# Decoding eight instead of four first-layer weight tiles ahead into result buffers, in a fused attention and two-layer kernel

## The chip, the cores and the metric

The kernel runs on 1 core of one Trainium2 chip. The metric is the device time of one execution in microseconds: 1045.17 us, the median of 3 runs (1044.94 to 1045.97).

## The reference

Three stages follow one another. The tokens are 4 batches of 448, the model width is 768 (12 heads of 64).

```python
scores = cap * np.tanh(scale * q @ k.T / cap)      # per batch and head
x = softmax(scores) @ v                            # 1792 x 768
h = np.maximum(x @ w_in, 0.0)                      # 768 -> 2048
x = (h * h) @ w_out                                # 2048 -> 768
# then 8 experts; each token goes to one, 224 tokens each, by its sorted gate logits
out[mask] = np.maximum(x[mask] @ w1[e], 0.0) @ w2[e]
```

All arrays are float32. The routing is greedy over all logits in falling order.

## The kernel before, in words

**Tiling.** Attention runs batch by batch, in 6 pairs of heads per batch (`attention`, from L234). Per pair, PE computes scores (L259, L261), ScalarE (ACT) takes tanh and exp (L263, L264), DVE or POOL adds up the sums (z, L271 to L279), PE multiplies by v into a PSUM tile U named aux (L286) and sums z over partitions (L295). Then comes the normalisation: for batches from 1 on ACT copies z (L298), DVE takes a reciprocal (L299) and multiplies U by it (L301). That last product is kept in `self.norms` for batch 0. There are two aux buffers, for U and for the sum of z in turn.

**The dense layer.** It works in split fp32: each operand is a high and a low part, and three products replace one (`hidden`, L434 to L436; `output`, L491 to L493). `hidden` goes over 16 tiles j of w_in, with 18 products for each tile in each of the 4 batches. For batch 0 the weights arrive as 64-bit words holding floats in a wider form. A tile goes through these steps:

1. `decode` (L351): SP's queue loads the words into one of 3 buffers raw (L356), and three DVE instructions (L360, L361, L362) make float32 of them in a buffer wf.
2. `split_weights` (L387): ACT copies the high part to wh (L391), and POOL (for every sixth tile DVE) subtracts for wl (L392). There are 4 buffers each of wh and wl.
3. PE uses wh and wl; SP's queue stores both to DRAM (L410) for the later batches.

`weights(n)` (L395) is called for tile n of the sequence that is just to be used. It has tiles up to n+3 loaded and decoded (for n below 4, FIRST tiles more) and tiles up to n+2 split. Tiles 0 to 15 are w_in's, and the 24 after them w_out's.

**The buffers of decoded tiles.** Tiles 3 to 2 + FIRST go to buffers g of the first layer's results, of which there are 16; all others take 3 buffers wf in turn:

```python
if 3 <= n < 3 + FIRST:
    wf = self.mp.tile([128, 2 * S], F32, name="g", bufs=NF)[:, :DM]
else:
    wf = self.wts.tile([128, DM], F32, name="wf", bufs=3)
with self.after(self.norms, WAIT[0], n):
    self.decode(wf, (self.wi if m == "i" else self.wo)[j], w)
```

**The order of the work.** A scheduler orders each engine's instructions ahead of time, by simulated readiness and, among ready ones, by the order in which the program traces them. `after` (L364) adds an edge: in the issue order of DVE, the decoding instructions of tile n come behind `norms[WAIT[0][n]]`, the last product (L301) of that pair of heads of batch 0. It holds for instructions on DVE alone; the load on SP's queue is not ordered by it. `run` traces attention of batch 0 first, then merges `hidden(0)` and `attention(1)` in small steps by their progress. From batch 2 on PE's order is as written; up to then the scheduler chooses it. Each engine executes its instructions strictly in the order built, SP's queue its transfers too.

Of the kernel before, what the change touches and what calls it, by code (L numbers as in the profile page):

```python
# [23 lines left out]
HP = NH // 2  # L24
KC = 4
KP = S // KC
WAIT = {3: 1, 4: 2, 5: 3, 6: 4, 7: 4, 8: 5, 9: 5, 10: 5}, {0: 8, 1: 12, 2: 16}
KB = S // 128
ND = DM // 128
DA = 4  # L30
# [18 lines left out]
AHEAD = 12  # L49
PLAIN = 4  # L50
EARLY = 6
FIRST = 4
WB = 4
START, MASK, VOTE, REST, GATHER, LIST = (7.7, 8.0), (1.85, 3.4), (1.0, 2.6), (0.86, 2.2), (11.0, 12.4), (6.0, 10.0)

# [35 lines left out]
class Kernel:  # L91
# [276 lines left out]
    def load_weights(self, n):  # L368
# [5 lines left out]
        if b == 0:  # L374
# [6 lines that stand above are left out]
# [14 lines left out]
    def weights(self, n):  # L395
        while self.loaded < min(n + 4 + (FIRST if n < 4 else 0), len(self.seq)):
            self.load_weights(self.loaded)
            self.loaded += 1
        while self.ready < min(n + 3, self.loaded):
            if self.seq[self.ready][0] == 0:  # L400
                with self.after(self.exps, WAIT[1], self.ready):
                    self.wtile[self.ready] = self.split_weights(*self.wtile[self.ready])
            self.ready += 1
        pair = self.wtile.pop(n)
        b, m, j = self.seq[n]
        if b == 0:
            w = DM if m == "i" else FF // OB
            self.cache[m, j] = [self.dram.tile([128, w], F32, name=f"w{m}{h}{j}") for h in "hl"]
            for t, c in zip(pair, self.cache[m, j]):
                self.nc.sync.dma_start(c, t[:, :w].bitcast(F32))  # L410
        return pair
# [622 lines left out]
```

## Time and profile before

| | |
|---|---|
| median of 3 runs | 1045.17 us |
| the profiled execution, its own time | 1046.55 us |
| its span in the profile | 1044.8 us |
| busy PE, DVE, ACT, POOL | 1030.5, 586.7, 468.6, 246.0 us |
| granted TensorE clock | 0.996 of full speed |

Times in the profile count from the span's start. PE is the matrix engine's products, PEld its weight loads, which overlap them; SPq is SP's queue of transfers. A row of the timeline gives start, duration, engine, line, operation, what is written from what, and the count of merged instructions; brackets give the engine's idle time just before and what ended it.

### The profile page before, as it was taken

The page shows a single profiled execution, that of the slowest core. Times are in us where ns is not written, and L with a number is a line of the kernel's source. Part 1 is how long each engine was busy: PE and PEld are TensorE (multiplying, and loading weights), DVE is VectorE, ACT ScalarE, POOL GpSimd, SP SyncE. Part 2 cuts the span into 40 slices and gives each one's busy share as a digit, 9 for nine tenths or more (in the row PEclk, how much of TensorE's full clock was granted, in tenths as well). Part 3 has the DMA queues.
Part 4 walks back from the last instruction along what each step waited for, and adds up shares of the span by engine and source line. Part 5 has one row for each costly group of instructions (what it writes and reads, how often), then busy time and mean ns, then how long its engine had stood idle before and what let it go on. Part 6 is the DMA issues. An engine that isn't in the chain of part 4 may idle for free.

```text
span 1044.8 us, 15693 instructions
## 1 busy us (share of the span) xinstructions
PE 1030.5 (99%) x5718; PEld 818.7 (78%) x5718; DVE 586.7 (56%) x1131; ACT 468.6 (45%) x725; POOL 246.0 (24%) x184
## 2 busy tenths in 40 slices
PE   9999999999999999999999999999999999999997
PEld 2246655777677777777888888888999999989997
DVE  5996899997222155556411225444637448677552
ACT  6868776544564633464544100101313224435542
POOL 0237684764221222222000100001220201021000
PEclk9999999999999999999999999999999999999999
DMA  7656767799655589987786268668567358467530
GB/s 283 221 219 240 254 213 240 238 318 348 222 180 190 161 291 336 388 297 283 260 308 220 89 199 289 196 191 266 184 210 256 107 184 281 166 204 235 181 120 27
DMA packets 102654, 237.59 MB, mean 227 GB/s; under 512 B 11121, under 2 KB 22033, under 8 KB 102577
## 3 DMA queue, kind: packets, MB, share of 16 engines
q1 hardware_dynamic: 87712, 219.65, 61.6%
q0 software_dynamic: 3424, 11.19, 3.6%
q10 hardware_dynamic: 11440, 5.75, 2.0%
q8 instruction: 45, 0.74, 0.3%
q14 instruction: 33, 0.26, 0.1%
HBM read 194.08 MB, written 42.47 MB: 226 GB/s over the span
## 4 chain that ended last, share of the span: by engine, by line
PE 85%; issue 10%; DVE 2%; ACT 1%; DMA 1%; POOL 1%; POOLq 0%; ACTq 0%
PE big L969 8%; PE acc L434 8%; PE acc L491 8%; PE acc L435 7%; PE acc L436 7%; PE acc L492 7%; PE acc L493 7%; PE aux L286 6%; PE acc L901 6%; PE big L259 5%; PE acc L908 2%; PE big L261 2%; PE aux L706 2%; PE aux L295 1%; PE aux L592 1%
## 5 line engine op out<-in xcount | busy, mean ns | idle before, releaser
L491 PE MATMUL acc<-g,wh 128*128 128x448 f32 x384 | 148.9, 388 | 0.0
L434 PE MATMUL acc<-xh,wh 128*128 128x448 f32 x384 | 146.3, 381 | 0.0
L492 PE MATMUL acc<-g,wh 128*128 128x448 f32 x384 | 139.9, 364 | 0.0
L435 PE MATMUL acc<-xl,wh 128*128 128x448 f32 x384 | 139.8, 364 | 0.0
L493 PE MATMUL acc<-g,wl 128*128 128x448 f32 x384 | 139.7, 364 | 0.0
L436 PE MATMUL acc<-xh,wl 128*128 128x448 f32 x384 | 139.2, 363 | 0.0
L969 PE MATMUL big<-wh,g 128*112 128x384 f32 x512 | 118.3, 342 | 0.0
L263 ACT ACTIVATE p<-big,isc 128x896 f32<-128x896 f32 x96 | 85.9, 907 | 40.6 <-PE big L259 40.0
L446 DVE TENSOR_TENSOR g<-r,g 128x448 fp32r<-128x448 f32 x58 | 40.6, 701 | 103.2 <-ACT g L445 102.9
L434 PEld LDWEIGHTS acc<-xh,wh 128*128 128x128 f32 x384 | 72.1, 188 | 30.6 <-issue 16.5
L264 ACT ACTIVATE p<-p,capt 128x896 f32<-128x896 f32 x96 | 89.2, 948 | 1.8
L813 POOL DMA_INDIRECT xg<-x,idx x32 | 32.0, 1000 | 245.6 <-DMA wh<-woh 128.3
L969 PEld LDWEIGHTS big<-wh,g 128*112 128x112 f32 x512 | 86.6, 175 | 0.4
L299 DVE RECIPROCAL z<-z 128x448 f32<-128x448 f32 x18 | 53.1, 2949 | 60.1 <-ACT z L298 60.1
L286 PE MATMUL aux<-p,v 128*64 128x448 f32 x384 | 84.8, 552 | 0.1
L491 PEld LDWEIGHTS acc<-g,wh 128*128 128x128 f32 x384 | 73.3, 191 | 11.3 <-issue 5.6
L435 PEld LDWEIGHTS acc<-xl,wh 128*128 128x128 f32 x384 | 72.2, 188 | 7.9 <-issue 3.5
L492 PEld LDWEIGHTS acc<-g,wh 128*128 128x128 f32 x384 | 72.4, 189 | 6.3 <-issue 2.2
L493 PEld LDWEIGHTS acc<-g,wl 128*128 128x128 f32 x384 | 72.0, 188 | 6.0 <-issue 0.7
L436 PEld LDWEIGHTS acc<-xh,wl 128*128 128x128 f32 x384 | 72.0, 188 | 5.8 <-issue 0.7
L441 ACT ACTIVATE r<-acc 128x448 f32<-128x448 f32 x64 | 34.8, 544 | 86.4 <-PE acc L436 86.4
L259 PE MATMUL big<-qk 64*128 64x448 f32 x288 | 71.4, 578 | 1.0 <-ACT p L263 1.0
(191 smaller groups left out, 1820.1 us busy)
## 6 DMA issues: line engine op xcount, KB each, us to landing
g<-w SPq DMA_DIRECT2D x62, 384.0 KB
wh<-wih SPq DMA_DIRECT2D x48, 384.0 KB
wl<-wil SPq DMA_DIRECT2D x48, 384.0 KB
wh<-woh SPq DMA_DIRECT2D x72, 256.0 KB
wl<-wol SPq DMA_DIRECT2D x72, 256.0 KB
wf<-w SPq DMA_DIRECT2D x33, 384.0 KB
raw<-w SPq DMA_DIRECT2D x33, 384.0 KB
raw<-w_in SPq DMA_DIRECT2D x16, 768.0 KB
```

The costliest lines, as they stand in the source:

```text
L259: nc.tensor.matmul(ps[:, s, :S], k[rows], q[rows], start=True, stop=True)
L263: nc.scalar.activation(p, ps[:, :n, :S], AF.Tanh, scale=self.isc)
L264: e = nc.scalar.activation(p, p, AF.Exp, scale=self.capt)
L286: nc.tensor.matmul(U[hp][s * 64:s * 64 + 64], vt[hp][:, c, s * 64:s * 64 + 64], P[hp, c][:, s if c < KB else 0], start=(c == 0), stop=(c = ...
L434: nc.tensor.matmul(ps, wh[:, d], xh, start=(d == 0), stop=False)
L435: nc.tensor.matmul(ps, wh[:, d], xl, start=False, stop=False)
L436: nc.tensor.matmul(ps, wl[:, d], xh, start=False, stop=(d == ND - 1))
L491: nc.tensor.matmul(ps, a, gh, start=(f == 0), stop=False)
L492: nc.tensor.matmul(ps, a, gl, start=False, stop=False)
L493: nc.tensor.matmul(ps, z, gh, start=False, stop=(f == NF - 1))
L901: nc.tensor.matmul(H[j], W[j][0][:, d], xs[:, d, 0].bitcast(F32), start=(d == 0), stop=(d == ND - 1))
L969: nc.tensor.matmul(acc[h][:, s, :DM // 2], l, r[:, s * (DM // 2):(s + 1) * (DM // 2)], start=(j == 0 and first), stop=(j == NF2 - 1 and last))
```

## The change

FIRST rises from 4 to 8. So tiles 3 to 10, not 3 to 6, are decoded into g buffers, and while the first four tiles are in use up to 11 tiles ahead, not 7, are loaded. The three wf buffers are then taken by tiles 0 to 2 and from 11 on (before: from 7 on). WAIT gets entries for tiles 11, 12 and 13: their decoding instructions too are issued behind `norms[5]`, the last L301 of batch 0, as those of tiles 8 to 10 are already.

```diff
-WAIT = {3: 1, 4: 2, 5: 3, 6: 4, 7: 4, 8: 5, 9: 5, 10: 5}, {0: 8, 1: 12, 2: 16}
+WAIT = {3: 1, 4: 2, 5: 3, 6: 4, 7: 4, 8: 5, 9: 5, 10: 5, 11: 5, 12: 5, 13: 5}, {0: 8, 1: 12, 2: 16}
...
-FIRST = 4
+FIRST = 8
```

## Rows read from the trace of the kernel before

**Rows 1.** The page, busy time of each engine over the span.

```profile
PE 1030.5 (99%) x5718; PEld 818.7 (78%) x5718; DVE 586.7 (56%) x1131; ACT 468.6 (45%) x725; POOL 246.0 (24%) x184
```

**Rows 2.** Busy time by stretch; then PE's weight loads of L434, 62 to 172 us.

```profile
core 0: us, PE busy (x) PEld busy (x) DVE busy (x) ACT busy (x) POOL busy (x), PEclk, DMA share, GB/s
62.00:172.00 110.00, 110.00 (x485) 66.85 (x484) 96.21 (x73) 80.97 (x120) 76.54 (x41) 1.00 0.66 226
80.00:100.00 20.00, 20.00 (x91) 13.82 (x89) 12.86 (x8) 18.02 (x29) 18.80 (x11) 1.00 0.65 242
100.00:120.00 20.00, 20.00 (x92) 11.79 (x89) 17.07 (x13) 14.63 (x22) 13.36 (x8) 1.00 0.78 274
...
L434 PEld LDWEIGHTS acc<-xh,wh 128*128 128x128 f32 x96 | 18.0, 188 | 15.6 <-issue 9.5 <-ACT wh L391 2.8 <-ACT p L263 0.7
```

**Rows 3.** Timeline of PE, 62 to 172 us: start, duration, engine, line.

```profile
62.13 0.47 PE L434 MATMUL acc<-xh,wh 128*128 128x448 f32 x1
62.44 0.36 PE L435 MATMUL acc<-xl,wh 128*128 128x448 f32 x1
...
63.44 0.36 PE L434 MATMUL acc<-xh,wh 128*128 128x448 f32 x1
63.73 0.97 PE L286 MATMUL aux<-p,v 128*64 128x448 f32 x4
...
91.44 1.72 PE L286 MATMUL aux<-p,v 128*64 128x448 f32 x6
...
119.02 0.47 PE L434 MATMUL acc<-xh,wh 128*128 128x448 f32 x1
...
171.06 0.47 PE L434 MATMUL acc<-xh,wh 128*128 128x448 f32 x1
```

**Rows 4.** Timeline of DVE, 75 to 125 us.

```profile
75.09 3.72 DVE L362 SCALAR_TENSOR_TENSOR wf<-raw,wf 128x768 int32<-128x768 int32 x2
83.40 2.95 DVE L299 RECIPROCAL z<-z 128x448 f32<-128x448 f32 x1 [4.60 <-ACT z L298]
...
87.18 0.61 DVE L301 TENSOR_TENSOR x<-aux,z 128x448 f32<-128x448 f32 x1
...
94.62 1.50 DVE L360 TENSOR_SCALAR wf<-raw 128x768 int32<-128x768 int32 x1 [2.95 <-POOL wl L392]
...
97.15 2.77 DVE L362 SCALAR_TENSOR_TENSOR wf<-raw,wf 128x768 int32<-128x768 int32 x1
...
101.99 0.55 DVE L360 TENSOR_SCALAR wf<-raw 128x768 int32<-128x768 int32 x1
...
103.57 0.97 DVE L362 SCALAR_TENSOR_TENSOR wf<-raw,wf 128x768 int32<-128x768 int32 x1
...
108.06 0.50 DVE L360 TENSOR_SCALAR wf<-raw 128x768 int32<-128x768 int32 x1
...
109.53 0.95 DVE L361 SCALAR_TENSOR_TENSOR wf<-raw,wf 128x768 int32<-128x768 int32 x1
110.51 2.75 DVE L362 SCALAR_TENSOR_TENSOR wf<-raw,wf 128x768 int32<-128x768 int32 x1
114.97 1.50 DVE L360 TENSOR_SCALAR wf<-raw 128x768 int32<-128x768 int32 x1 [1.70 <-POOL wl L392]
...
118.34 1.78 DVE L362 SCALAR_TENSOR_TENSOR wf<-raw,wf 128x768 int32<-128x768 int32 x1
...
124.30 0.56 DVE L360 TENSOR_SCALAR wf<-raw 128x768 int32<-128x768 int32 x1 [1.74 <-POOL wl L392]
```

**Rows 5.** Timeline of POOL, 96 to 102 us.

```profile
96.18 2.92 POOL L273 TENSOR_TENSOR z<-p,p 128x896 f32<-128x896 f32 x1 [0.48 <-ACT p L264]
99.05 2.54 POOL L392 TENSOR_TENSOR wl<-wf,wh 128x768 fp32r<-128x768 f32 x1
```

**Rows 6.** Timeline of SP's queue, the loads of raw for w_in, 76 to 101 us.

```profile
77.00 2.16 SPq L356 DMA_DIRECT2D raw<-w_in  x2
...
99.94 0.33 SPq L356 DMA_DIRECT2D raw<-w_in  x1
```

## The prediction

> **What bounds the kernel now.** I read the busy table first: the matrix engine (PE) is busy for 1030.5 of 1044.8 us [rows 1]. The change touches only the input weights of the first dense layer, so the stretch that matters runs from the first product with w_in, at 62.13 us, to the last ones at about 172 us [rows 3]. The table by stretch shows PE busy for 110.00 of these 110 us, and for the whole of each 20 us slice in it; the vector engine (DVE) has 12.86 of 20 and 17.07 of 20, and POOL 18.80 of 20 in the slice from 80 us on [rows 2]. The list of waits, cut to this stretch and to PE, is empty. So in this stretch PE waits for nobody, and what DVE does there is hidden unless it comes too late.
>
> A busy share can flatter PE, so I checked the timeline of single products. Between L435 at 62.44 and L434 at 63.44 lie five starts, one every 0.20 us, and each holds a weight load of 0.188 us [rows 2, 3]: within a run of such products PE is full. By the Trainium skill, Perfetto Trace Analysis, Identifying the Most-Contended Engine, matmul busy time is no measure of the distance to the roofline, and the busy share of weight loads is. By that rule the 66.85 of 110.00 us of weight loads [rows 2] would leave 43 us open. The rows speak against using it here: the 0.188 of 0.20 us is full by the rule's own measure, and the share falls because attention's fp32 products hold PE longer for each load. The only irregularity that I find between starts is at the changes from one kind of product to the other; that is the faster rival below.
>
> **What the limit on decoding is now.** A w_in tile is decoded by three DVE instructions. Tiles 0 to 2 and from 7 on use three buffers named wf, so tile n from 10 on waits until tile n-3 has been split. The timeline of DVE shows it: tile 10 begins at 94.62 after 2.95 us of idling for POOL's wl, tile 13 at 114.97 and tile 14 at 124.30 likewise, and tile 11 at 101.99 directly behind the split of tile 8, which ends at 99.05 + 2.54 = 101.59 [rows 4, 5].
>
> **The change, part by part.**
> 1. Tiles 7 to 10 go to g buffers, tiles 11 to 13 to the three wf buffers, free since tiles 0 to 2 were split. So tiles 10, 11, 12 and 13 lose the wait for a split. Tile 14 reuses tile 11's buffer, as it does now, and still waits for the same split, after which it begins at 124.30 [rows 4]. From tile 14 on, the ring of buffers is the old one, and nothing later is decoded earlier. Four decodes move. Tile 7 was in no wait; it only changes its address.
> 2. Work on DVE: none is added. The four moved decodes took 97.15 + 2.77 - 94.62 = 5.30 (tile 10), 103.57 + 0.97 - 101.99 = 2.55 (tile 11), 0.50 + 0.95 + 2.75 = 4.20 (tile 12, with other work between its three instructions) and 118.34 + 1.78 - 114.97 = 5.15 us (tile 13), 17.2 us together [rows 4]. Tile 11's 2.55 us is the price without company; the others ran beside POOL. Bounds for the four: 4 x 2.55 = 10.2 and 4 x 5.30 = 21.2 us. I take 17.2, for POOL is as busy where they go [rows 2].
> 3. What the earlier decode brings PE: nothing. Tile 8 was split at 101.59, and its first product came at 119.02 [rows 3, 5]: 17 us of slack, and the split, not the decode, is what the next tile waits for; it is paced by the products that free wh and wl.
> 4. DMAs: the raw loads of tiles 13 to 16 each follow the decode three before them, so SP issues them earlier (tile 13 now at 99.94) [rows 6]. The order on issue binds DVE instructions only, not the loads. Behind an early raw load on SP stand the stores of split weights, and v and qk loads. The stores free wh and wl, where the 17 us of slack is the cover; the next heads' loads are a whole head ahead. I cost this at nothing; should one of them wait as long as the first pair of raw loads took to issue, 2.16 us [rows 6], the slack covers it.
> 5. The hidden results shift by four g buffers. A result of tile j from 8 on now takes a buffer that held tile 3 to 10, all of them split before tile 11 is; its first use, tile 8's result, comes after 119.02 [rows 3], when tile 3 is long split. I cost it at nothing.
> 6. The order on DVE: tiles 8 to 13 are held behind the last product with a reciprocal of the first attention, so attention of batch 0 is unharmed. They are not held behind anything of batch 1. Loads 8 to 11 are traced before all of batch 1, and 12 and 13 before its first normalisation, so the scheduler prefers them. This is the only place where I see a loss.
>
> The sum: 0 on the path. Against the profiled execution's own 1046.55 us (span 1044.8 [rows 1]) that gives 1046.55; it lies 1.38 us above the median of the runs, so I forecast the median, 1045.2 us. A measurement of this kernel tells some 0.2%, 2.1 us, from no change.
>
> **Rivals.**
> *Slower: the first normalisation of batch 1 waits behind decodes.* Its reciprocal starts at 83.40 and the product L301 ends at 87.18 + 0.61 = 87.79; that frees a PSUM buffer, and the next head's product with v starts on PE at 91.44 [rows 3, 4]. The slack is 3.65 us. DVE is free from 75.09 + 3.72 = 78.81, where tile 9 ends [rows 4]. If tiles 10, 11 and 12 stand ahead of the reciprocal, it starts at 78.81 + 5.30 + 2.55 + 4.20 = 90.86, 7.46 us late: PE, whose order is fixed when the program is built, stands for 7.46 - 3.65 = 3.8 us, and gets none of it back. With two decodes ahead (86.7, 3.3 us late) nothing shows; with four it is 9.0 us; at the price without company three hide (86.5) and four cost 2.0 us. It decides when the third decode is ahead. For it: the trace order; POOL's 18.80 of 20 us. Against: raw tile 12 cannot be fetched before tile 9 is decoded, so it lands after the reciprocal is ready; and the scheduler places PE's products by its own DVE times, so it can put more hidden products in front. I take three: 1045.2 + 3.8 = 1049.0 us. Chance 0.20.
> The row that carries the long prices is tile 10's third instruction, 2.77 us from 97.15, where tile 11's took 0.97; POOL ran z from 96.18 to 99.10 and wl from 99.05 [rows 4, 5]. By the Trainium skill, SBUF — State Buffer, Who interferes with whom, a DVE instruction with two SBUF inputs contends with a POOL instruction that reads SBUF, and the second to start is blocked for the whole of the other. The trace agrees; it is a rule against this change.
>
> *Faster: PE changes kind less often.* Between 62.13 and 171.06 PE starts 29 runs of split-weight products between fp32 ones [rows 3]. Entering one costs 62.44 - 62.13 - 0.20 = 0.11 us, leaving one 63.73 - 63.44 - 0.20 = 0.09, together 0.20. With more tiles ready the scheduler could place runs of a whole tile (18 products): 288 products in 16 runs, 13 fewer, 2.6 us, 1042.6 us. Against: the tiles are ready 17 us ahead already, and the interleaving follows the written merge of the two streams. Chance 0.13.
>
> *The decodes don't move:* the program holds them back elsewhere (raw ring, order). Then the time is 1045.2 as well; it is inside the forecast.
>
> **How the numbers follow.** No change 0.66, faster 0.13, slower 0.21 (the slower rival with 0.01 for a mishap elsewhere). Likeliest time 1045.2. Own range of that case: plus or minus 1.2 us, from six entries more or fewer. The range given reaches to both rivals' prices: 1042.6 to 1049.2; outside it lies the four-decode case, 1045.2 + 9.0 = 1054.2.
>
> **What would show it.** Right: tiles 10 to 13 decoded by about 100 us instead of 120; DVE idles for POOL's wl at tile 14 alone; tile 14 still near 124; PE full from 62 to 172; about 29 runs. Wrong on the slow side: PE idle before L286 near 91 us, released by DVE L301, and the reciprocal of batch 1's first head starting after 90. Wrong on the fast side: clearly fewer runs, or the work of this stretch ending before 170.

## The result and the profile after

The changed kernel takes 1051.86 us (median of 6 runs, 1051.37 to 1053.70), the kernel before beside it 1045.06 us (6 runs, 1044.55 to 1045.97). The ratio is 1.0069, with a 95% interval of 1.0058 to 1.0080: 6.8 us slower, above the forecast and above the upper end of the range. The profiled execution took 1052.11 us with a span of 1050.3 us, 5.5 us longer than that of before.

The page, busy time of each engine, and from its part 5 the group of the first product of a triple, with its idle time behind the second bar:

```profile
PE 1030.3 (98%) x5718; PEld 818.1 (78%) x5718; DVE 587.9 (56%) x1131; ACT 468.8 (45%) x725; POOL 245.7 (23%) x184
...
L434 PE MATMUL acc<-xh,wh 128*128 128x448 f32 x384 | 147.1, 383 | 4.8 <-ACT r L441 4.8
```

No engine has more instructions than before, and none has over 1.2 us more busy time [rows 1]. PE has the same 1030 us to do and stands still in between: 4.8 us before L434, put down to ACT's L441. Busy time by stretch shows where:

```profile
62.00:172.00 110.00, 104.51 (x451) 63.21 (x450) 88.93 (x67) 74.87 (x109) 70.54 (x38) 0.98 0.64 216
80.00:100.00 20.00, 19.08 (x86) 12.36 (x82) 19.86 (x11) 10.99 (x18) 17.40 (x8) 1.00 0.83 270
100.00:120.00 20.00, 16.07 (x67) 10.83 (x67) 11.96 (x11) 15.31 (x24) 9.54 (x6) 0.91 0.78 269
```

PE, busy for all of these stretches before [rows 2], is idle for 5.5 of the 110 us. DVE has gone from 12.86 to 19.86 of 20 us in the slice from 80 on: it is full there, and it has been given work of later tiles. The granted clock, 1.00 before, is 0.91 in the slice from 100 on.

The list of waits says what ended the idle time. PE, 62 to 180 us, in total, times, longest; then ACT, 80 to 106 us:

```profile
PE acc L434 <- ACT r L441: 4.8, 1, 4.8
PE acc L435 <- DVE xl L348: 0.6, 1, 0.6
...
ACT r L441 <- DVE g L446: 11.6, 1, 11.6
```

So there are two steps back from PE: PE waited for ACT, and ACT had itself waited 11.6 us for one DVE instruction, L446. The timeline of DVE shows what stood ahead of it:

```profile
79.86 5.97 DVE L362 SCALAR_TENSOR_TENSOR g<-raw,g 128x768 int32<-128x768 int32 x3
85.75 2.48 DVE L360 TENSOR_SCALAR wf<-raw 128x768 int32<-128x768 int32 x1
88.27 1.79 DVE L361 SCALAR_TENSOR_TENSOR wf<-raw,wf 128x768 int32<-128x768 int32 x1
90.10 2.75 DVE L362 SCALAR_TENSOR_TENSOR wf<-raw,wf 128x768 int32<-128x768 int32 x1
92.77 1.49 DVE L360 TENSOR_SCALAR wf<-raw 128x768 int32<-128x768 int32 x1
94.29 1.78 DVE L361 SCALAR_TENSOR_TENSOR wf<-raw,wf 128x768 int32<-128x768 int32 x1
96.11 2.46 DVE L362 SCALAR_TENSOR_TENSOR wf<-raw,wf 128x768 int32<-128x768 int32 x1
98.49 0.55 DVE L360 TENSOR_SCALAR wf<-raw 128x768 int32<-128x768 int32 x1
98.96 2.94 DVE L299 RECIPROCAL z<-z 128x448 f32<-128x448 f32 x1
101.82 0.89 DVE L361 SCALAR_TENSOR_TENSOR wf<-raw,wf 128x768 int32<-128x768 int32 x1
102.63 0.61 DVE L446 TENSOR_TENSOR g<-r,g 128x448 fp32r<-128x448 f32 x1
103.16 0.61 DVE L301 TENSOR_TENSOR x<-aux,z 128x448 f32<-128x448 f32 x1
```

Tiles 8 to 10 are decoded interleaved and end with the first row, at 85.83. Tile 11 takes the next three rows, tile 12 the three after them, and tile 13's first two instructions surround the first reciprocal of batch 1. Only then comes L446 of tile 1, the low part of the second hidden result (tiles count from 0). In the kernel before, the same L446 stood between the reciprocal and L301:

```profile
86.27 0.99 DVE L446 TENSOR_TENSOR g<-r,g 128x448 fp32r<-128x448 f32 x1
```

ACT had finished its operand at 86.18 there and at 86.33 here, so DVE is 16.4 us late with it.

ACT runs nothing between these two rows of its timeline; the second waits for that L446:

```profile
90.94 0.83 ACT L391 CAST wh<-g 128x768 fp32r<-128x768 f32 x1
103.33 0.55 ACT L441 ACTIVATE r<-acc 128x448 f32<-128x448 f32 x1 [11.56 <-DVE g L446]
```

PE's timeline around the stop; the row at 107.01 is the last of the nine products that follow it:

```profile
98.72 0.36 PE L436 MATMUL acc<-xh,wl 128*128 128x448 f32 x1
103.93 0.74 PE L434 MATMUL acc<-xh,wh 128*128 128x448 f32 x1 [4.85 <-ACT r L441]
104.47 0.57 PE L435 MATMUL acc<-xl,wh 128*128 128x448 f32 x1
104.84 0.57 PE L436 MATMUL acc<-xh,wl 128*128 128x448 f32 x1
...
107.01 0.37 PE L436 MATMUL acc<-xh,wl 128*128 128x448 f32 x1
```

The first and the last of the same nine products in the kernel before, tile 5's first being the row at 97.89:

```profile
97.89 0.36 PE L434 MATMUL acc<-xh,wh 128*128 128x448 f32 x1
...
99.49 0.36 PE L436 MATMUL acc<-xh,wl 128*128 128x448 f32 x1
```

**The chain.** r has two buffers (the code: `name="r", bufs=2`). Tile 3's r needs the buffer that tile 1's L446 still has to read, so ACT's L441 of tile 3 waits 11.56 us. L441 is what empties tile 3's PSUM accumulator, and there are two of those, so the first product of tile 5 can't start. It starts 5.21 us after the product before it, where 0.20 us is the spacing.

**The bill**, each product of after against the same one of before. At 98.72 PE is 1.03 us late (its product stands at 97.69 in before). At 103.93 it is 6.04 late (97.89): the stop cost 5.01. From there to 107.01 eight steps take 3.08 us, 1.60 in before: 1.48 us more, because products now start 0.37 us apart, not 0.20. At 107.01 it is 7.52 late (99.49), and at the last w_in product of batch 0 7.69 (179.86 against 172.17). Of the 1.03 us, 0.15 stand there already at the product at 74.84 (74.69 in before); the rest stems from a second late DVE product, xl (L348, waited for 0.64 us at 77.6), and what is reordered beside it. In a second profile of this kernel, below, that wait is absent and the stop is 5.25 us. Of the 7.69 us, 5.5 are left at the end of the span; where the other 2.2 go is not the same in the two profiles, and stays unexplained.

The order of PE's instructions is the same as before, but for two neighbouring products near 77 us that stand two places earlier. That is the point on which everything below turns.

### The profile page after: what moved, and what is told of

Read it like the earlier page. It is cut to its first block, busy times and chain, and to the rows that moved or that the text cites. A ratio compares the mean times of both kernels' runs of the same rounds, so it can differ in the third digit from the quotient of the medians.

```text
span 1050.3 us, 15688 instructions
## 1 busy us (share of the span) xinstructions
PE 1030.3 (98%) x5718; PEld 818.1 (78%) x5718; DVE 587.9 (56%) x1131; ACT 468.8 (45%) x725; POOL 245.7 (23%) x184
## 4 chain that ended last, share of the span: by engine, by line
PE 81%; issue 8%; DVE 5%; ACT 2%; DMA 2%; POOL 1%; another core or an unknown queue 0%; POOLq 0%; SPq 0%; ACTq 0%
PE big L969 9%; PE acc L491 8%; PE acc L434 7%; PE acc L492 7%; PE acc L493 7%; PE acc L435 7%; PE acc L436 7%; PE acc L901 6%; PE aux L286 5%; PE big L259 4%; PE acc L908 3%; PE aux L706 2%; PE aux L295 1%; PE big L261 1%; DMA raw<-w_in 1%
## 5 line engine op out<-in xcount | busy, mean ns | idle before, releaser
L434 PE MATMUL acc<-xh,wh 128*128 128x448 f32 x384 | 147.1, 383 | 4.8 <-ACT r L441 4.8
L446 DVE TENSOR_TENSOR g<-r,g 128x448 fp32r<-128x448 f32 x58 | 40.7, 702 | 118.5 <-ACT g L445 118.2
L434 PEld LDWEIGHTS acc<-xh,wh 128*128 128x128 f32 x384 | 72.4, 189 | 35.9 <-issue 17.0
L299 DVE RECIPROCAL z<-z 128x448 f32<-128x448 f32 x18 | 53.1, 2949 | 57.5 <-ACT z L298 57.5
L286 PE MATMUL aux<-p,v 128*64 128x448 f32 x384 | 84.8, 552 | 0.1
L441 ACT ACTIVATE r<-acc 128x448 f32<-128x448 f32 x64 | 34.8, 544 | 98.7 <-PE acc L436 86.4
L259 PE MATMUL big<-qk 64*128 64x448 f32 x288 | 71.2, 576 | 1.7 <-ACT p L263 1.7
```

Of the source, the lines that this page charges most:

```text
L259: nc.tensor.matmul(ps[:, s, :S], k[rows], q[rows], start=True, stop=True)
L286: nc.tensor.matmul(U[hp][s * 64:s * 64 + 64], vt[hp][:, c, s * 64:s * 64 + 64], P[hp, c][:, s if c < KB else 0], start=(c == 0), stop=(c = ...
L434: nc.tensor.matmul(ps, wh[:, d], xh, start=(d == 0), stop=False)
```

## Experiments

The theory at the start, A: decodes ahead of L446 of tile 1 on DVE, lengthened by POOL, hold r, hence acc, hence PE. Rivals: the late normalisation (L299, L301) holds PE, as the prediction's slower rival said; the new buffers or the bigger lead in loads cost time by themselves. Each ratio is against the kernel before on the same chip, whose median was 1041.7 to 1044.4 us there. All edits are on the changed kernel unless said otherwise.

**The buffers without the early decoding.** Tiles 3 to 10 go to g buffers, but the lead stays that of before.

```diff
-        while self.loaded < min(n + 4 + (FIRST if n < 4 else 0), len(self.seq)):
+        while self.loaded < min(n + 4 + (4 if n < 4 else 0), len(self.seq)):
```

> Edit: FIRST = 8 for the buffers, but only four tiles more are loaded ahead, as in the kernel before; so tiles 7 to 10 use g buffers and tiles 11 to 13 find wf free, and yet decodes 10 and later are traced behind the hidden results of the tiles before them. Theory A: DVE's order has L446 of the second tile right behind decode 8, ACT and PE never wait: same as the kernel before within 1 us. If the freed buffers themselves (the earlier loads, the places in g) cost something, 2 us or more slower.

1042.97 us, ratio 1.0007 (0.9998 to 1.0017). L446 of tile 1 is at 89.42, and PE waits for nothing between 62 and 180 us. The addresses are harmless; it is the tracing of decodes 8 to 11 ahead of all of batch 1 that moves them to the front of DVE's queue. The three new entries of WAIT do nothing: built without them, the changed program is the same.

**How many tiles ahead.** FIRST is 6, then 7; and the changed kernel again, for its profile on another chip.

```diff
-FIRST = 8
+FIRST = 6
```

> Edit: FIRST = 6 in place of 8, so two tiles fewer are decoded ahead; DVE's order then has decodes 8 to 11 ahead of L446 of the second hidden tile, no longer tile 12 and the start of 13. Theory A: L446 comes some 6 us earlier, which is more than PE's wait of 4.8 us, so no wait for acc remains; the smaller loss of 0.9 us before 80 us (xl L348 behind decodes) stays: 1045 to 1046.5. Rival B: L301 comes 6 us earlier too, near 97, still 9 us later than in the kernel before, so part of the loss stays: 1047 to 1050. Rival C: fewer loads early, 1047 to 1050.

> Edit: FIRST = 7. DVE's order has decodes 8 to 12 ahead of L446 of the second hidden tile, but not the start of 13. Theory A (the results of the second and third tile wait on DVE behind decodes, their two buffers r hold up ACT and that PE): L446 comes 1 to 3 us earlier than in the changed kernel, so PE's wait shrinks from 4.8 to between 2 and 4 us and brings the lower clock again; 3 to 6 us slower than before. With FIRST = 6 nothing was lost: the loss sets in with the decode of tile 12. Rival C (SP's queue): about 3.5 us per step, so also 3.5 us.

> The changed kernel itself, beside the kernel before on the same chip, as the measure for the other runs of this chip. All theories: some 7 us slower than the kernel before, PE's wait of 4.8 us for L441 and the stretch at the lower clock as in its first profile.

FIRST 6: 1041.80 us, 0.9997 (0.9987 to 1.0006). FIRST 7: 1048.41 us, 1.0060 (1.0044 to 1.0077). FIRST 8: 1050.26 us, 1.0074 (1.0057 to 1.0091). L446 and L441 in the timelines, then PE at tile 5's first product, with the stop where there is one; first FIRST 6:

```profile
95.48 1.81 DVE L446 TENSOR_TENSOR g<-r,g 128x448 fp32r<-128x448 f32 x1
97.21 0.61 DVE L301 TENSOR_TENSOR x<-aux,z 128x448 f32<-128x448 f32 x1
97.38 0.55 ACT L441 ACTIVATE r<-acc 128x448 f32<-128x448 f32 x1 [5.76 <-DVE g L446]
98.35 0.36 PE L434 MATMUL acc<-xh,wh 128*128 128x448 f32 x1
```

FIRST 7:

```profile
100.81 0.56 DVE L446 TENSOR_TENSOR g<-r,g 128x448 fp32r<-128x448 f32 x1
102.06 0.74 PE L434 MATMUL acc<-xh,wh 128*128 128x448 f32 x1 [3.94 <-ACT r L441]
```

FIRST 8 a second time:

```profile
103.53 0.74 PE L434 MATMUL acc<-xh,wh 128*128 128x448 f32 x1 [5.25 <-ACT r L441]
```

A step, not a slope. From L446's end to tile 5's first product there are 0.69 us in the changed kernel (103.24 to 103.93), and in before that product starts at 97.89; so L446 may end as late as 97.20. It ended at 87.26: about 10 us of slack. With FIRST 6 it ends at 97.29. Tile 5 begins at 98.35 in that profile, so L446 is 0.37 us inside what is allowed there, and nothing shows. With FIRST 7 it ends at 101.37 and PE stops for 3.94 us. The same run speaks against the late normalisation: with FIRST 6, L301 ends at 97.82, 10 us later than in before (87.79 by [rows 4]), and PE waits for nothing.

**Without POOL's company.** For the first two pairs of heads of batch 1 the sums z are left out: a fill with 1.0 in place of L273, and no L275 and L279.

```diff
-                    nc.gpsimd.tensor_add(z, P[hp, 0], p)
-            elif c == 2:
+                    nc.gpsimd.memset(z, 1.0) if b == 1 and hp < 2 else nc.gpsimd.tensor_add(z, P[hp, 0], p)
+            elif c == 2 and (b != 1 or hp > 1):
...
-            elif c == KB and b:
+            elif c == KB and b and (b != 1 or hp > 1):
```

> Edit: the changed kernel without the adding up of the softmax sums on POOL for the first two pairs of heads of batch 1 (a constant is written instead; this part of the computation is left out). The order on DVE stays. Theory A with POOL as the cause of the long decodes: decodes 8 to 12, which took 26 us beside POOL where 2.5 us each would be 13, get some 5 us shorter, L446 of the second tile comes near 97 us instead of 102.6, and PE's wait of 4.8 us shrinks to 0 to 1: 1045 to 1047.5 us. Rival D (the decodes are long for another reason, such as waiting for raw loads): they keep their lengths, 1051 to 1053.

1041.73 us, 1.0002 (0.9993 to 1.0012): the whole loss is gone. The order on DVE and on PE is that of the changed kernel; only durations differ. First, busy time by stretch in the changed kernel (columns as above), then the same stretch here and DVE's rows of tile 12:

```profile
79.00:99.00 20.00, 20.00 (x90) 12.70 (x88) 19.86 (x13) 11.99 (x20) 17.40 (x8) 1.00 0.78 250
```

```profile
79.00:99.00 20.00, 20.00 (x92) 13.77 (x89) 15.47 (x14) 16.48 (x26) 8.39 (x5) 1.00 1.01 360
...
85.28 1.51 DVE L360 TENSOR_SCALAR wf<-raw 128x768 int32<-128x768 int32 x1
86.83 0.96 DVE L361 SCALAR_TENSOR_TENSOR wf<-raw,wf 128x768 int32<-128x768 int32 x1
87.82 0.96 DVE L362 SCALAR_TENSOR_TENSOR wf<-raw,wf 128x768 int32<-128x768 int32 x1
...
93.14 0.61 DVE L446 TENSOR_TENSOR g<-r,g 128x448 fp32r<-128x448 f32 x1
93.84 0.55 ACT L441 ACTIVATE r<-acc 128x448 f32<-128x448 f32 x1 [3.39 <-DVE g L446]
```

With POOL at 8.39 of 20 us instead of 17.40, tile 11's decode takes 0.89 + 2.49 + 0.96 = 4.34 us and tile 12's 3.43, where they took 7.02 and 5.73. Tiles 8 to 10 end earlier too, at 78.57 instead of 85.83. L446 ends at 93.75, 9.5 us earlier and inside the slack. So the decodes in front of L446 alone are not enough; their lengthening beside POOL is a necessary part. SP's queue has the order of the changed kernel here, so the earlier loads don't cost the 7 us by themselves either. By the Trainium skill, SBUF — State Buffer, Who interferes with whom, a DVE instruction with two SBUF inputs shares a port with a GpSimd instruction that reads SBUF, a tensor_scalar can come to hold that port too, and one with a single input outside those modes does not contend. The traces agree: in the changed kernel L360, L361 and L362 take 0.55, 0.89 and 0.94 us with POOL idle (98.49, 101.82 and 103.70) and up to 2.48, 1.79 and 2.75 beside it, while the reciprocal takes 2.94 us with POOL idle (98.96) and 2.95 beside POOL's sums (83.40 in before) [rows 4].

**More room for r.** In batch 0 r takes the unused buffers of another tile, seven instead of two.

```diff
-            r = mp.tile([128, S], F32, name="r", bufs=2)
+            r = self.tp.tile([128, S], F32, name="xt") if b == 0 else mp.tile([128, S], F32, name="r", bufs=2)
```

> Edit: the changed kernel, with the hidden result r of batch 0 in 7 buffers instead of 2; the order of the instructions on each engine stays that of the changed kernel. Theory A (two buffers r: DVE's subtraction L446 of the second hidden tile stands behind five decodes, so ACT's L441 of the fourth tile waits 11.6 us, so PE waits 4.8 us for a PSUM buffer acc, and then runs some 1.5 us at the lower clock): both go, 1045 to 1046.5 us, although L446 comes as late as before, near 102 us. Rival B (the late normalisation, L299 and L301 of batch 1's first heads, is what costs): they stay late, 1051 to 1053. Rival C (loads issued earlier on SP's queue delay stores and the loads of q, k and v): SP's order stays, 1051 to 1053.

1046.68 us, 1.0049 (1.0032 to 1.0066). L446 is as late as before, at 103.02, but ACT's wait for it and PE's for L441 are gone. In their place PE waits for the next things in DVE's queue:

```profile
107.85 0.47 PE L436 MATMUL acc<-xh,wl 128*128 128x448 f32 x1 [1.96 <-DVE wl L392]
...
104.30 0.97 PE L295 MATMUL aux<-z,ones 128*64 128x448 f32 x4 [0.32 <-DVE x L301]
```

So the chain through r is real, but cutting it gives back only a third of the loss: the expectation was too good. (The profiled execution is the fastest of the four, 1044.57 us. PE's waits between 62 and 180 us, 2.9 us in all, are those of this execution; for the other three, at 1046.57 to 1047.33, there is no trace.) DVE is late as a whole, and wl of tile 6, which is DVE's by the rule of every sixth tile, is the next victim.

**The same, and wl of tile 6 on POOL.**

```diff
-            self.wtile[n] = (wf, w, nc.gpsimd if n % 6 else nc.vector, self.wts, WB)
+            self.wtile[n] = (wf, w, nc.gpsimd if n % 6 or n == 6 else nc.vector, self.wts, WB)
...
-            r = mp.tile([128, S], F32, name="r", bufs=2)
+            r = self.tp.tile([128, S], F32, name="xt") if b == 0 else mp.tile([128, S], F32, name="r", bufs=2)
```

> Edit: the changed kernel with 7 buffers r for batch 0 (as in the first run of this study) and the split of tile 6 on POOL instead of DVE, so that two of the three things that PE was seen to wait for in DVE's queue are taken out of it; DVE's decodes stay, PE's order stays. Theory A2: with r alone 4.7 us were left, of which the profile showed 2.0 us of waiting for wl of tile 6, 0.3 for L301 and 0.9 before 80 us; now 0.5 to 2.5 us slower than before. If the queue of DVE as a whole is not the cause: still 4 to 5 us slower.

1045.96 us, 1.0017 (1.0007 to 1.0027). One wait of PE is left between 62 and 180 us, 0.66 us for xl. With L446 still at 103.01, the loss is down from 0.74% to 0.17%, on another chip: r's buffers and that wl account for most of it.

**L446 of tile 1 on POOL.** If only this instruction is the matter, POOL can do it.

```diff
-            (nc.gpsimd if b == 0 and j % 3 == 0 else nc.vector).tensor_sub(gl, r, gh.bitcast(F32))
+            (nc.gpsimd if b == 0 and (j % 3 == 0 or j == 1) else nc.vector).tensor_sub(gl, r, gh.bitcast(F32))
```

> Edit: the changed kernel, with L446 of the second hidden tile alone on POOL instead of DVE; every other instruction stays where it is. Theory A: POOL takes it at about 89 us, L441 of the fourth tile follows at once, PE's wait of 4.8 us and the low clock go: 1045 to 1047.5 us (the third tile's L446, still on DVE behind the decodes, may hold the fifth tile a little). Rival B: L301 stays near 103 us, 1051 to 1053. Rival C: 1051 to 1053.

1049.60 us, 1.0077 (1.0060 to 1.0093): no gain, and the expectation missed. ACT, then PE:

```profile
107.63 0.54 ACT L441 ACTIVATE r<-acc 128x448 f32<-128x448 f32 x1 [8.94 <-DVE g L446]
108.23 0.74 PE L434 MATMUL acc<-xh,wh 128*128 128x448 f32 x1 [3.85 <-ACT r L441]
```

The wait only moves one tile on: now it is tile 4's L441 that waits, for tile 2's L446, which DVE runs at 105.32.

**Only a late L446.** The kernel before, with a pad of five DVE instructions after which L446 of tiles 1 and 2 is ordered. Nothing is decoded earlier.

```diff
-            (nc.gpsimd if b == 0 and j % 3 == 0 else nc.vector).tensor_sub(gl, r, gh.bitcast(F32))
+            if b == 0 and j == 1:
+                pad = self.tp.tile([128, S], F32, name="xt")
+                nc.vector.tensor_scalar(pad, r, 1.0, None, op0=OP.add)
+                for i in range(4):
+                    last = nc.vector.reciprocal(pad, pad)
+            with self.tc.issue_after(last.ins) if b == 0 and 0 < j < 3 else nullcontext():
+                (nc.gpsimd if b == 0 and j % 3 == 0 else nc.vector).tensor_sub(gl, r, gh.bitcast(F32))
```

> Edit: the kernel before, with an addition and four reciprocals on a spare tile on DVE (some 12.5 us), and L446 of the second and third hidden tile ordered behind the last of them; the normalisation of the first pair of heads, the split of tile 6 and all loads keep their places, and no decode is moved. Theory A: L446 of the second tile comes near 103 us, L441 of the fourth tile waits for it, PE waits 4 to 6 us for acc and then runs at the lower clock: 5 to 8 us slower than the kernel before. Rival B (late normalisation) and rival C (SP's queue): no loss, within 1 us of the kernel before.

1040.96 us, 0.9988 (0.9978 to 0.9997). L446 of both tiles runs at 101.73, nearly as late as in the changed kernel, and PE loses nothing; the expected loss was wrong, and A as it stood with it. PE's timeline shows why:

```profile
98.33 1.72 PE L286 MATMUL aux<-p,v 128*64 128x448 f32 x8
99.89 0.92 PE L295 MATMUL aux<-z,ones 128*64 128x448 f32 x4
100.74 1.02 PE L259 MATMUL big<-qk 64*128 64x448 f32 x4
101.69 1.02 PE L261 MATMUL big<-qk 128*128 128x448 f32 x2
102.64 1.72 PE L286 MATMUL aux<-p,v 128*64 128x448 f32 x8
104.29 0.47 PE L434 MATMUL acc<-xh,wh 128*128 128x448 f32 x1
```

The order built has 6 us of attention here, and tile 5 starts behind it, at 104.29. In the changed kernel tile 5 is next. So the theory had to be revised, to A2: a late L446 costs time only where PE's order was built for an early one. The likely reason, not shown: the pad's reciprocals keep their length beside POOL (2.93 to 2.95 us), so that a scheduler could foresee them, while the decodes of 7.02 and 5.73 us came out longer than it reckoned.

**Attention first.** If A2 holds, an order that puts attention ahead of tile 5 by hand should remove the wait for L441, and show what else DVE holds.

```diff
+            if b == 0 and j == 5:
+                yield 8.0
```

> Edit: the changed kernel, with the merge made to hand out attention's next products ahead of the sixth hidden tile; on PE four products with v, two sums of z and three scores (some 4 us) now stand before that tile's first product, DVE's order up to the second and third tile's L446 stays. Theory A (a late L446 costs by itself): the hidden results come as late as in the changed kernel, so 6 to 8 us slower than before. Theory A2 (it costs because PE's fixed order has the product that needs the buffer next, as the order was built for shorter decodes): the wait for L441 shrinks to about 1 us, but the sums of z need the aux buffer that L301 frees, which ends near 103.7 in the changed kernel: PE waits there for some 3 us instead, and 4 to 6 us slower than before.

1052.76 us, 1.0084 (1.0066 to 1.0102): 8.3 us slower, above the 4 to 6 that A2 gave and the 6 to 8 that A gave, so the time does not decide between them. The waits do: as A2 had it, the wait for L441 is gone from PE, though ACT still waits 11.56 us, and PE waits for L301 instead. PE's timeline:

```profile
103.31 1.32 PE L295 MATMUL aux<-z,ones 128*64 128x448 f32 x4 [3.63 <-DVE x L301]
104.83 1.86 PE L259 MATMUL big<-qk 64*128 64x448 f32 x4 [0.20 <-ACT p L263]
107.11 1.86 PE L261 MATMUL big<-qk 128*128 128x448 f32 x2 [0.43 <-ACT p L263]
```

The attention that now comes first needs L301, which is late as well: the PSUM buffer that it frees is wanted by the next pair's sum of z (L295). Hidden layer and attention are both held up by DVE's queue, so this order is no way out.

**The pad, with PE's order pinned.** The run with the pad alone shows no price for a late L446, since the order moved. Here the kernel with the pad also has the second half of the products with v of the second pair ordered behind tile 5's seventh product.

```diff
-                nc.tensor.matmul(ps, wh[:, d], xh, start=(d == 0), stop=False)
+                mm = nc.tensor.matmul(ps, wh[:, d], xh, start=(d == 0), stop=False)
+                if b == 0 and j == 5 and d == 2:
+                    self.fifth = mm
...
-                pv(hp - 1, 2, 4)
+                with self.tc.issue_after(self.fifth.ins) if b == 1 and hp == 2 else nullcontext():
+                    pv(hp - 1, 2, 4)
```

> Edit: the padded kernel of the run before (the kernel before, with 12.5 us of extra work on DVE ahead of L446 of the second and third hidden tile), and in addition the products with v of the second pair of heads are held on PE behind the sixth tile's seventh product, so that PE's order around the late result is again that of the kernel before. Theory A2: L446 comes near 102, as in the padded kernel, and now PE waits for L441 from 98.5 on, 4 to 5 us, and then runs at the lower clock: 5 to 8 us slower than before, where the padded kernel lost nothing. If neither L446 nor the order is the cause: same as the padded kernel, within 1 us of before.

1045.79 us, 1.0023 (1.0010 to 1.0035): 1.4 us slower, where 5 to 8 were expected. The scheduler put other fp32 products, L295, L259, L261 and the third pair's first L286, in front from 97.95 us on; tile 5 began at 104.11 and PE waited for nothing. The order of before was not obtained, so this tells nothing on A2.

**The faster rival.** The kernel before, with the first batch's hidden layer merged by whole tiles instead of half tiles: 19 runs of split-weight products instead of 28 between 62 and 173 us.

```diff
-                if d == 2:
+                if d == 2 and b:
...
-            yield 1.7
+            yield 1.7 if b else 3.4
```

> Edit: the kernel before, with the merge of the first hidden layer's batch 0 handing out a whole tile (18 products) at a time instead of half a tile; PE then changes 16 times fewer between split-weight and fp32 products, eight entries and eight exits. The faster rival of the prediction prices an entry and an exit at 0.20 us together: 8 x 0.20 = 1.6 us faster than before (0.15 per cent), if nothing else comes late. Against it: if the price of a change is only a shift within the pipeline, no difference; if whole tiles make attention's products late for ACT, up to 1 us slower.

1042.50 us, 1.0005 (0.9996 to 1.0014), where 1.6 us less was expected: fewer changes of kind bring nothing that can be measured in the total. In this one profile the stretch ended earlier (last w_in product at 170.32 us, 172.17 in before on another chip), but at 199.74 PE stands still for 0.94 us, waiting for ACT's L298, which it does not in before. So the price of 0.20 us for a run is neither shown nor excluded; the time that it would give back did not reach the end.

## Why the prediction was wrong

**What held.** The matrix engine was full, and DVE's work was hidden *unless it comes too late*, as the first paragraph said. Step 1 held: from tile 14 on the ring is the old one, and tile 14 was decoded at 129.96, though with L446 ahead of it, not a wait for POOL's wl. Step 3 held: earlier decodes brought PE nothing (FIRST 6, ratio 0.9997). Step 5 held: the shifted buffers are harmless (ratio 1.0007). Step 4 held in the main, but not to nothing: in the changed kernel DVE stood 1.79 us for a raw load at 72.90, ahead of the xl (L348, 76.64 against 71.75 in before) for which PE waited 0.64 us. In the second profile DVE stood 0.89 us for that load, and PE did not wait for xl.

**The step that failed** is step 6, which saw DVE's new order and put it at nothing ("0 on the path", where 6.8 us were measured), and the price of the rival built on it. Step 6 named the right place, batch 1's work on DVE behind decodes of batch 0, and the rival the right sign, the lock between DVE and POOL, and that a threshold decides (FIRST 6 costs nothing, FIRST 7 costs 0.60%). But the forecast stood on the other side, with a chance of 0.20 for the rival, for four reasons:

1. *The wrong victim.* The rival let L301 hold the next product with v, at 91.44 [rows 3], with 3.65 us of slack. In the changed kernel that product ran at 92.47, while L301 came at 103.16: it doesn't need L301's buffer. Products with v and sums of z don't simply take the two aux buffers in turn: a pair's products with v take the buffer of the sum before them, which ACT's L298 frees, and its sum of z (L295) takes the one that L301 frees, as the row with attention first shows. In before that L295 ran at 103.44, 15.65 us after L301's end, so the 7.46 us of the rival would have cost nothing by this path; that its sign came true was luck, as far as this path goes. So of the two signs that the prediction named for the slow side, the late reciprocal appeared and the idling before L286 didn't. The victim was L446, whose 10 us were the smaller slack; the prediction never listed it, though it stood in DVE's timeline between the reciprocal and L301. A list of all that DVE does between 80 and 105 us, each with its reader and the number of its buffers, would have led from L446 to two r buffers, two accumulators and PE.
2. *The price of a decode.* Step 2 took 2.55 to 5.30 us for a tile, and the rival 12.05 us for tiles 10 to 12. Tiles 11 and 12 alone took 12.75 us. In before, tiles stand between other work; put back to back under POOL's 17.4 of 20 us, almost each of their instructions meets a POOL instruction.
3. *The start.* The rival had DVE free from 78.81. There tile 10 was interleaved with 8 and 9, and they ended at 85.83. With the prices this made the reciprocal 15.56 us late (98.96 against 83.40 in [rows 4]) where 7.46 were supposed; 6.0 of the 8.1 us between them are tiles 11 and 12 (12.75 where 2.55 + 4.20 were supposed). L446's end was 15.98 us late (103.24 against 87.26); 9.94 of them were slack, and the other 6.04 are PE's delay at 103.93.
4. *The counterweights.* That raw tile 12 "lands after the reciprocal is ready" doesn't help, since DVE's order is fixed and what is behind a decode waits, ready or not. That the scheduler "can put more hidden products in front" did not happen: it moved PE's order for the pad, but here PE's order stayed the same.

The size of the rival, 3.8 us, was too small beside the 6.8 measured for one more reason: it charged a stop for its length alone. The 5.01 us cost another 1.48 in slower products right behind them. The upper end of the range stood on the rival's price, and so lay too low.

**The faster rival** did not come about here: the changed kernel has 28 runs of split-weight products, as many as before (the prediction counted 29). Nor is its price confirmed: with 9 runs fewer the ratio was 1.0005.

**What stays open.** That a late L446 under exactly the old order costs the full 5 us without any decode moved was not achieved. So A2 rests on the pad, whose order differs in more than one place. That the scheduler reckoned with shorter decodes is inferred from the unchanged order and from the pad; its own figures are not known here. None of these kernels beats the kernel before by more than the 0.2% that counts as a difference here.

## What to carry to other kernels

Where each engine's order is fixed ahead of time, work that is moved forward on an engine with idle time delays everything queued there behind it. So list every instruction that is passed, follow each through the number of its buffers to the engine that bounds the kernel, and work out its slack; the smallest decides, and below it the cost is zero (here 10 us, with a step between 6 and 7 tiles). Price the moved work by its longest rows beside its neighbour on the shared port, not by a mean, for back to back it meets that neighbour all the time.

## What the hardware showed

A stop of TensorE costs more than its length. After 4.85 us without a product, products start 0.37 us apart (104.47, 104.84) where 0.20 is usual; 448 columns in 0.37 us are the lower of the two levels, 1.2 GHz, and the granted clock of the slice is 0.91. From 106.71 on two steps are 0.30, and then the usual spacing returns: 1.48 us in all. With attention first, a stop of 3.63 us and two short ones behind it were followed by such products until 110.6 us.

The lengthening of DVE beside POOL is mutual: POOL's L273 took 2.85 us at 84.97 beside tile 11's decode, and 2.12 us at 83.55 in before beside the reciprocal.
